# Loading one tile transposed by DMA instead of transposing it on TensorE, at the start of a gated attention and feed-forward kernel

## The chip, the cores and the metric

The kernel runs on one core of a Trainium2 chip. The metric is device microseconds of one execution; medians of several executions are given with their range. The whole program takes about 274 us, and the change touches its first 8 us, so most effects below are some tenths of a microsecond, or about a thousandth of the time.

## The reference

```python
x = A_x                                             # 2048 x 640, bf16
g = sigmoid((x * gate_w).sum(-1, keepdims=True))
# A: linear attention, 32 heads of 20
q, k, v = split(x @ wqkv)                           # wqkv 640 x 1920
phi = lambda t: where(t > 0, t + 1, exp(t)) + 1e-6
o = (phi(q) @ (phi(k).T @ v)) / (phi(q) @ sum(phi(k)))      # per head
a = o @ wo
# B: gated feed-forward, F = 1728
b = (gelu(x @ w_gate) * (x @ w_up)) @ w_down
out = g * a + (1 - g) * b
```

## The kernel before

x is cut into 16 tiles of 128 rows. Keys and queries need x transposed (`xT`), 128 columns (one chunk `k` of 5) at a time. Tiles 0 and 1 are loaded plainly and transposed on TensorE (`T`, through PSUM and a VectorE copy). Tiles 2 to 15 come transposed by DMA (`load_xT`).

```python
NXN = 2          # tiles transposed on TensorE
NQ = 4           # tiles whose keys and queries are computed apart, at the start
# ... cut
P.op("act", lambda e: e.dma_start(touch[...], ...))      # a tiny first DMA
load_x(0)                    # SyncE's queue, as all without "act"
load_wk(0)
load_x(1, "act")             # ScalarE's queue
load_wk(1)
load_wk(3)
P.op("act", lambda e: e.activation(eg[:, 0:1], zero, ACT.Exp), ...)
load_wk(2, "act")
load_wk(4, "act")
P.op("dve", lambda e: e.memset(gw_sb, 0.0), writes=[r_gw])
dma_in(gw_sb[0:5, :], gate_w..., [r_gw], eng="act")
for i in range(NXN, NQ):
    load_xT(i)               # DMA transpose, SyncE's queue
for k in range(KC):
    load_wq(k)
for i in range(NQ, NT):
    load_xT(i)
# ... cut: the rest of x, the feed-forward weights

# TensorE, in this order (warm(n, w): n matmuls of w columns on constants)
warm(5, 512); warm(1, 128)
T(0, [0], 7); T(0, [1, 2, 3, 4], 6)
warm(6, 128)
KM(0, [0])                   # keys of tile 0, chunk 0: 512 + 128 columns
T(1, [0], 7); T(1, [1, 2, 3, 4], 6)
warm(3, 128)
KM(1, [0])
for k in (1, 2, 3):
    KM(0, [k]); KM(1, [k])
gate_col()
KM(0, [4]); KM(1, [4])
# keys of tiles 2 and 3, queries of tiles 0 to 3
# ... cut
```

Then come keys and queries of tiles 4 to 15 together. Each tile's PSUM result is turned into phi by ScalarE (exp) and VectorE (min and add, then add and max, for keys in two parts):

```python
def phi(half, dst, r_dst, banks, cuts):          # in KQ(i), i = 4 to 15
    P.op("act", exp of 640 columns, reads=banks, ...)
    if half: P.op("act", tanh of one column, ...)
    P.op("dve", min and add, ...)
    for c0, c1, bk in cuts:
        P.op("dve", add and max, reads=bk + [r_e[m]], writes=[r_dst])
```

After tile 15 TensorE starts the products of keys and x ("k-v products" here), summed over the 16 tiles. Their steady part starts with line 599.

Of the kernel before, what the change touches and what calls it, by code (L numbers as in the profile page):

```python
# [20 lines left out]
EPS = 1e-6  # L21
XW = 656

NXN = 2
NQ = 4


# [135 lines left out]
def bass_gated_mix__linear_attn_block__geglu_ffn__prompt_kernel(  # L163
# [63 lines left out]
    with (  # L227
# [8 lines left out]
        with contextlib.ExitStack() as stack:  # L236
            dma_sems = [stack.enter_context(nc.semaphore("s_in%d" % i)) for i in range(n_dma_in)]

            P = _Plan(["pe", "act", "dve", "pool", "sp"])
# [9 lines left out]
            def new_dma_key():  # L249
                k = "in%d" % dma_next[0]  # L250
                dma_next[0] += 1
                return k

            def v16(o, n):
                return pool[:, o:o + n]
# [10 lines left out]
            xT = v16(R_XT, KC * S).rearrange("p (k s) -> p k s", k=KC)  # L266

            wkq = v16(R_WK, KC * WW).rearrange("p (k w) -> p k w", k=KC)
            wk = wkq[:, :, 0:640]
# [38 lines left out]
            r_xT = [P.sb("xT%d" % i, R_XT, R_XT + KC * S) for i in range(NT)]  # L308
            r_xTa = [P.sb("xTa%d" % i, R_XT, R_XT + S) for i in range(NXN)]
            r_wk = [P.sb("wk%d" % k, R_WK + k * WW, R_WK + k * WW + 640) for k in range(KC)]  # L310
# [29 lines left out]
            def dma_in(dst, src, writes, reads=(), eng="sp"):  # L340
                P.op(eng, lambda e, dst=dst, src=src: e.dma_start(dst, src),
                     reads=reads, writes=writes, dma=new_dma_key())
# [3 lines left out]
            def load_x(i, eng="sp"):  # L346
                dma_in(x_aug[:, i, 0:640], A_x[0, i * 128:(i + 1) * 128, :], [r_xn[i]], eng=eng)

            def load_wk(k, eng="sp"):
                dma_in(wk[:, k, :], A_wqkv[k * 128:(k + 1) * 128, 640:1280], [r_wk[k]], eng=eng)  # L350

            def load_wq(k, eng="sp"):
                dma_in(wq[:, k, 0:640], A_wqkv[k * 128:(k + 1) * 128, 0:640], [r_wq[k]], eng=eng)
# [3 lines left out]
                 writes=[P.res("touch")], dma=new_dma_key())  # L357
            load_x(0)
            load_wk(0)
            load_x(1, "act")  # L360
            load_wk(1)
            load_wk(3)

            zero = nc.const_aps.tensor(0.0, (128, 1), F32)
            P.op("act", lambda e: e.activation(eg[:, 0:1], zero, ACT.Exp), writes=[r_eg[0]])
            load_wk(2, "act")
            load_wk(4, "act")
            P.op("dve", lambda e: e.memset(gw_sb, 0.0), writes=[r_gw])
            dma_in(gw_sb[0:5, :], gate_w.rearrange("(k p) -> k p", p=128), [r_gw], eng="act")
            def load_xT(i, after=()):  # L370
                P.op("sp", lambda e: e.dma_start_transpose(xT[:, :, i * 128:(i + 1) * 128],
                                                           A_x[0, i * 128:(i + 1) * 128, :]),
                     reads=list(after), writes=[r_xT[i]], dma=new_dma_key())

            for i in range(NXN, NQ):
                load_xT(i)
            for k in range(KC):
                load_wq(k)
            for i in range(NQ, NT):
                load_xT(i)  # L380
            dma_in(x_aug[:, NXN:8, 0:640],
                   A_x[0, NXN * 128:8 * 128, :].rearrange("(i p) w -> p i w", p=128), r_xn[NXN:8])
            dma_in(x_aug[:, 8:NT, 0:640],
# [4 lines left out]
            for c in range(NHC):  # L388
# [9 lines left out]
                 reads=[r_ones], writes=[r_ident])  # L398
# [16 lines left out]
            def warm(count, n):  # L415
                def fn(e):
                    last = None
                    for w in range(count):
                        last = e.matmul(ps[:, 4, 0:n], one_l, one_r[:, 0:n], start=True, stop=True)  # L419
                    return last  # L420
                P.op("pe", fn, writes=[bank[4]])
# [4 lines left out]
            def slot(n):  # L426
                return SLOTS[n % 4]

            def T(i, ks, tb):
                def fn(e):  # L430
                    last = None
                    for n, k in enumerate(ks):
                        last = e.transpose(psb[:, tb, n * 128:(n + 1) * 128],
                                           x_aug[:, i, k * 128:(k + 1) * 128], ident)
                    return last
                P.op("pe", fn, reads=[r_xn[i], r_ident], writes=[bank[tb]])
                P.op("dve", lambda e: e.tensor_copy(
                    xT[:, ks[0]:ks[-1] + 1, i * 128:(i + 1) * 128],
                    psb[:, tb, 0:len(ks) * 128].rearrange("p (k s) -> p k s", k=len(ks))),
                    reads=[bank[tb]], writes=[r_xTa[i] if ks[0] == 0 else r_xT[i]])  # L440
# [4 lines left out]
            def KM(n, ks):  # L445
                i = seq[n][1]
                b0, b1 = slot(n)

                def fn(e):
                    last = None  # L450
                    for k in ks:
                        lhs = xT[:, k, i * 128:(i + 1) * 128]
                        e.matmul(ps[:, b0, :], lhs, wk[:, k, 0:512], start=(k == 0), stop=(k == KC - 1))  # L453
                        last = e.matmul(ps[:, b1, 0:128], lhs, wk[:, k, 512:640],  # L454
                                        start=(k == 0), stop=(k == KC - 1))
                    return last
                P.op("pe", fn, reads=[r_xTa[i] if i < NXN and ks == [0] else r_xT[i]] + [r_wk[k] for k in ks],
                     writes=[bank[b0], bank[b1]])
# [37 lines left out]
            def gate_col():  # L496

                P.op("pe", lambda e: e.matmul(ps[:, 7, 0:5], gw_sb, ident[:, 0:5], start=True, stop=True),
                     reads=[r_gw, r_ident], writes=[bank[7]])
                P.op("dve", lambda e: e.tensor_copy(wq[:, :, 640:641], ps[:, 7, 0:5].unsqueeze(2)),  # L500
                     reads=[bank[7]], writes=[r_gcol])
# [3 lines left out]
            warm(1, 128)  # L505
            T(0, [0], 7)
            T(0, [1, 2, 3, 4], 6)
            warm(6, 128)
            KM(0, [0])
            T(1, [0], 7)  # L510
            T(1, [1, 2, 3, 4], 6)
            warm(3, 128)
            KM(1, [0])
            for k in (1, 2, 3):
                KM(0, [k])
                KM(1, [k])
            gate_col()
            for k in (4,):
                KM(0, [k])
                KM(1, [k])  # L520
            ALLK = list(range(KC))
            for n in range(2 * NQ):
                if n in (2, 3):
# [45 lines left out]
            for i in range(NQ, NT):  # L569
                KQ(i)  # L570
                if i == 4:
                    late_constants()
            P.op("dve", lambda e: e.tensor_scalar(gg, eg, 0.5, 0.5, ALU.mult, ALU.add),
                 reads=r_eg, writes=[r_g])
            P.op("dve", lambda e: e.tensor_scalar(omg, eg, -0.5, 0.5, ALU.mult, ALU.add),
                 reads=r_eg, writes=[r_omg])
# [7 lines left out]
                 reads=[r_omg], writes=[r_od], dma=new_dma_key())  # L584
# [44 lines left out]
            def ME(g):  # L629
# [6 lines left out]
                for c in cs:  # L636
# [8 lines left out]
                 reads=r_pk[0:2], writes=[r_tmp[0]])  # L645
            for i in range(2, NT):
                P.op("dve", lambda e, i=i: e.tensor_tensor(zacc, zacc, pk[i], ALU.add),  # L647
                     reads=[r_tmp[0], r_pk[i]], writes=[r_tmp[0]])
# [283 lines left out]
```

## Time and profile before

| | us |
|---|---|
| median of the first three executions | 273.77 (273.75 to 274.64) |
| span of the traced execution | 272.7 |
| TensorE busy | 269.8 (99%) |

The profile's page gives busy times in its first part and, in its fourth, the chain of work that ended last, as shares of the span.

```profile
PE 269.8 (99%) x1379; PEld 128.7 (47%) x1379; DVE 141.0 (52%) x249; ACT 75.9 (28%) x132; POOL 30.0 (11%) x28
...
PE 98%; DVE 1%; ACT 0%; issue 0%; DVEq 0%
```

TensorE is nearly always busy and nearly all of the chain. The timeline view shows the start: start in us, duration, engine, line, operation. Line 433 is a transpose, 419 a warm-up, 453 the first half of a keys matmul pair.

```profile
3.02 0.73 PE L433 MATMUL ps<-pool 128*128 128x128 bf16 x5
...
3.55 0.85 PE L419 MATMUL ps<-const-bfloat16-1.0 128*128 128x128 bf16 x6
...
4.52 0.50 PE L453 MATMUL ps<-pool 128*128 128x512 bf16 x1
...
4.91 0.44 PE L433 MATMUL ps<-pool 128*128 128x128 bf16 x5
...
5.19 0.34 PE L419 MATMUL ps<-const-bfloat16-1.0 128*128 128x128 bf16 x3
...
5.45 0.39 PE L453 MATMUL ps<-pool 128*128 128x512 bf16 x1
...
5.74 0.38 PE L453 MATMUL ps<-pool 128*128 128x512 bf16 x1
...
7.93 0.38 PE L453 MATMUL ps<-pool 128*128 128x512 bf16 x1
```

Tile 1's transposes and three warm-ups stand in the stream from 4.91 to 5.45. From there, pairs follow every 0.27 us, and 7.93 is the first keys matmul of tile 2. For the cost of a DMA transpose, the view by windows compares 16 to 20 us, mostly transposes, with 25 to 47 us, bulk loads. The columns are the stretch, its length, the busy time and instructions of TensorE, its weight loads, VectorE, ScalarE and GpSimd, the clock, the DMA engines' busy share and GB/s.

```profile
16.00:20.00 4.00, 4.00 (x24) 2.11 (x22) 3.32 (x8) 1.50 (x4) 0.00 (x0) 1.00 0.61 125
25.00:47.00 22.00, 22.00 (x124) 11.85 (x122) 19.37 (x41) 11.76 (x24) 0.00 (x0) 1.00 1.02 365
```

### The profile page before, as it was taken

How to read it: one execution, taken by the hardware profiler on the slowest of the kernel's cores; microseconds unless marked ns; L12 is line 12 of the kernel's file. 1: busy time of each engine (PE TensorE's matmuls, PEld its weight loads, DVE VectorE, ACT ScalarE, POOL GpSimd, SP SyncE). 2: the span in 40 equal slices, each digit the busy share in tenths (PEclk: the TensorE clock that was granted, in tenths of full speed). 3: DMA queues.
4: the chain of work that ended last, by engine and by line, in shares of the span. 5: the costliest groups of instructions: out<-in, count | busy, mean ns of one | idle time of the engine just before them, and what ended most of it. 6: DMA issues, size and time to landing. Idle time of an engine off the chain costs nothing.

```text
span 272.7 us, 3467 instructions
## 1 busy us (share of the span) xinstructions
PE 269.8 (99%) x1379; PEld 128.7 (47%) x1379; DVE 141.0 (52%) x249; ACT 75.9 (28%) x132; POOL 30.0 (11%) x28
## 2 busy tenths in 40 slices
PE   8999999999999999999999999999999999999997
PEld 4555555444445444444444444444444444444444
DVE  2688989897233335999999999634210000000200
ACT  2455554210422453232222233224011122121021
POOL 5000000003240002242332422000000000000000
DMA  7976999300210011612121231263031110110221
GB/s 211 210 111 137 384 402 377 52 3 18 59 22 0 23 50 50 190 36 49 26 48 24 48 48 28 60 218 108 2 77 38 41 38 19 38 41 19 58 60 38
DMA packets 42208, 23.61 MB, mean 87 GB/s; under 512 B 31567, under 2 KB 40783, under 8 KB 42063
## 3 DMA queue, kind: packets, MB, share of 16 engines
q1 hardware_dynamic: 41717, 22.89, 31.2%
q10 hardware_dynamic: 474, 0.49, 0.5%
q8 instruction: 11, 0.18, 0.3%
q14 instruction: 6, 0.05, 0.1%
HBM read 13.83 MB, written 2.63 MB: 60 GB/s over the span
## 4 chain that ended last, share of the span: by engine, by line
PE 98%; DVE 1%; ACT 0%; issue 0%; DVEq 0%
PE ps L703 41%; PE ps L867 23%; PE ps L542 11%; PE ps L599 6%; PE ps L846 4%; PE ps L453 2%; PE ps L468 2%; PE ps L814 2%; PE ps L681 2%; PE ps L602 1%; PE ps L419 1%; PE ps L827 1%; PE ps L724 1%; PE ps L742 0%; PE ps L469 0%; PE ps L454 0%
## 5 line engine op out<-in xcount | busy, mean ns | idle before, releaser
L703 PE MATMUL ps<-pool 128*128 128x512 bf16 x520 | 113.7, 379 | 0.0
L703 PEld LDWEIGHTS ps<-pool 128*128 128x128 bf16 x520 | 50.5, 98 | 60.0
L867 PE MATMUL ps<-pool 128*128 128x512 bf16 (+2 forms) x306 | 62.7, 367 | 0.0
L709 ACT ACTIVATE pool<-ps 128x512 f32<-128x512 f32 x52 | 31.0, 597 | 73.1 <-PE ps L703 73.1
L711 DVE TENSOR_TENSOR pool<-ps,pool 128x512 bf16<-128x512 f32 x52 | 34.7, 689 | 31.7 <-PE ps L703 30.3
L867 PEld LDWEIGHTS ps<-pool 128*128 128x128 bf16 x306 | 29.2, 98 | 33.4 <-issue 0.4
L850 DVE TENSOR_TENSOR pool<-ps,pool 128x512 bf16<-128x512 f32 x4 | 2.8, 692 | 61.5 <-PE ps L846 61.5
L542 PE MATMUL ps<-pool 128*128 128x512 bf16 (+1 forms) x180 | 32.7, 344 | 0.0
L757 POOL TENSOR_TENSOR pool<-pool 128x640 f32<-128x640 bf16 x16 | 22.4, 1404 | 72.9 <-DVE pool L759 65.9
L874 ACT ACTIVATE pool<-ps,pool 128x512 bf16<-128x512 f32 (+1 forms) x16 | 10.9, 680 | 68.6 <-PE ps L867 68.6
L542 PEld LDWEIGHTS ps<-pool 128*128 128x128 bf16 x180 | 17.6, 98 | 15.0
L561 DVE SCALAR_TENSOR_TENSOR pool<-ps,pool 128x128 bf16<-128x128 f32 (+2 forms) x36 | 21.7, 603 | 2.5 <-DVE pool L558 0.5
L552 ACT ACTIVATE pool<-ps 128x640 bf16<-128x640 f32 x24 | 16.9, 703 | 16.1 <-DVE pool L561 9.0
L599 PE MATMUL ps<-pool 128*128 128x512 bf16 x78 | 19.4, 379 | 0.0
L767 DVE TENSOR_TENSOR pool<-pool 128x640 bf16<-128x640 bf16 x16 | 13.2, 825 | 0.6
L765 DVE TENSOR_SCALAR pool<-pool 128x32 f32<-128x32 f32 x16 | 12.8, 801 | 0.6
L759 DVE TENSOR_REDUCE pool<-pool 128x32 f32<-128x640 f32 x16 | 12.9, 809 | 0.0
L647 DVE TENSOR_TENSOR pool<-pool 128x640 f32<-128x640 f32 x14 | 11.6, 826 | 0.5
L846 PE MATMUL ps<-pool 128*128 128x512 bf16 x52 | 11.6, 380 | 0.0
L649 POOL PARTITION_ALL_REDUCE pool<-pool x1 | 4.0, 3971 | 61.2 <-DVE pool L647 61.2
L599 PEld LDWEIGHTS ps<-pool 128*128 128x128 bf16 x78 | 7.0, 98 | 7.2
L558 DVE TENSOR_SCALAR pool<-pool 128x640 bf16<-128x640 bf16 x24 | 7.8, 325 | 2.0 <-ACT pool L552 0.8
(70 smaller groups left out, 127.4 us busy)
## 6 DMA issues: line engine op xcount, KB each, us to landing
out_dram<-pool SPq DMA_DIRECT2D x19, 128.0 KB, 1.7
pool<-in_B_w_gate_dram SPq DMA_DIRECT2D x1, 2080.0 KB, 14.4
pool<-in_B_w_up_dram SPq DMA_DIRECT2D x1, 2080.0 KB, 19.0
pool<-in_A_wqkv_dram SPq DMA_DIRECT2D x8, 160.0 KB, 3.2
pool<-in_A_x_dram SPq DMA_DIRECT2D x1, 1280.0 KB, 8.8
pool<-in_B_w_down_dram SPq DMA_DIRECT2D x1, 1120.0 KB, 6.3
pool<-omg_row SPq DMA_DIRECT2D x1, 1024.0 KB, 4.8
pool<-in_A_x_dram SPq DMA_DIRECT2D x1, 960.0 KB, 5.9
```

The source lines that it names most:

```text
L542: last = e.matmul(ps[:, b + p, 0:c1 - c0], xT[:, k, i * 128:(i + 1) * 128], wkq[:, k, c0:c1], start=(k == 0), stop=(k == KC - 1))
L552: P.op("act", lambda e: e.activation(e_buf[m], ps_flat[:, o:o + 640], ACT.Exp), reads=banks, writes=[r_e[m]])
L561: P.op("dve", lambda e, c0=c0, c1=c1: e.scalar_tensor_tensor(dst[:, c0:c1], ps_flat[:, o + c0:o + c1], 1.0 + EPS, e_buf[m][:, c0:c1], ALU. ...
L599: last = e.matmul(ps[:, b, :], pk[i][:, c * 128:(c + 1) * 128], x_aug[:, i, 0:512], start=(i == 0), stop=(i == NT - 1))
L703: last = e.matmul(ps[:, b, :], w[:, k, fc * 128:(fc + 1) * 128], xT[:, k, j * 512:(j + 1) * 512], start=(k == 0), stop=(k == KC - 1))
L709: P.op("act", lambda e: e.activation(ge[n], ps[:, gb, :], ACT.Gelu_apprx_tanh), reads=[bank[gb]], writes=[r_ge[n]])
L711: P.op("dve", lambda e: e.tensor_tensor(hT[fc][:, j * 512:(j + 1) * 512], ps[:, ub, :], ge[n], ALU.mult), reads=[bank[ub], r_ge[n]], write ...
L757: P.op("pool", lambda e: e.tensor_tensor(tmp[n], pq[i], z_b, ALU.mult), reads=[r_pq[i], r_zb], writes=[r_tmp[n]])
L759: P.op("dve", lambda e: e.tensor_reduce(den[n], tmp[n].rearrange("p (h d) -> p h d", h=32), AX.X, ALU.add), reads=[r_tmp[n]], writes=[r_de ...
L767: P.op("dve", lambda e: e.tensor_tensor(pq[i].rearrange("p (h d) -> p h d", h=32), pq[i].rearrange("p (h d) -> p h d", h=32), den[n].unsqu ...
L846: last = e.matmul(ps[:, b, :], wd[:, fc, 512:640], hT[fc][:, j * 512:(j + 1) * 512], start=False, stop=(fc == NFC - 2), skip_group_check=True)
L867: last = e.matmul(ps[:, pb, 0:c1 - c0], lhs, rhs, start=False, stop=(q == len(rows) - 1), skip_group_check=True)
```

## The change

The intent: TensorE bounds the kernel, so take tile 1's transposes and the three warm-ups that follow them from its stream, and let the DMA do them. Tile 1's transpose goes third on SyncE's queue. wk chunks 1 and 2 go to ScalarE's queue, which no longer carries x tile 1. TensorE runs tile 0's keys for chunks 0 to 2 first, while tile 1 arrives.

```diff
-NXN = 2
+NXN = 1
@@ loads (SyncE's queue unless "act")
             load_x(0)
             load_wk(0)
-            load_x(1, "act")
-            load_wk(1)
+            load_xT(1)
             load_wk(3)
+            load_wk(4)
+            load_wk(1, "act")
+            load_wk(2, "act")
 ... the exponential that loads ScalarE's table
-            load_wk(2, "act")
-            load_wk(4, "act")
-            for i in range(NXN, NQ):
+            for i in range(2, NQ):
                 load_xT(i)
@@ TensorE
             T(0, [0], 7)
             T(0, [1, 2, 3, 4], 6)
-            warm(6, 128)
-            KM(0, [0])
-            T(1, [0], 7)
-            T(1, [1, 2, 3, 4], 6)
-            warm(3, 128)
-            KM(1, [0])
-            for k in (1, 2, 3):
+            warm(2, 128)
+            for k in range(3):
                 KM(0, [k])
+            for k in range(3):
                 KM(1, [k])
+            KM(0, [3])
+            KM(1, [3])
             gate_col()
-            for k in (4,):
-                KM(0, [k])
-                KM(1, [k])
+            KM(0, [4])
+            KM(1, [4])
```

(The helper `load_xT` moves up and helpers get an unused argument.) VectorE loses two copies, because T(1) is gone. And tile 1 of x is now moved twice: the later products need it untransposed too, so the bulk load of x that begins at tile `NXN` grows from 960 to 1120 KB (issued at about 25 us).

More of the change, by code (lines that the diff above doesn't have):

```diff
@@ L347, in load_x, with load_wk, load_xT @@
                 dma_in(x_aug[:, i, 0:640], A_x[0, i * 128:(i + 1) * 128, :], [r_xn[i]], eng=eng)
-            def load_wk(k, eng="sp"):
-                dma_in(wk[:, k, :], A_wqkv[k * 128:(k + 1) * 128, 640:1280], [r_wk[k]], eng=eng)
+            def load_wk(k, eng="sp", after=()):
+                dma_in(wk[:, k, :], A_wqkv[k * 128:(k + 1) * 128, 640:1280], [r_wk[k]], reads=after, eng=eng)
+            def load_xT(i, after=()):
+                P.op("sp", lambda e: e.dma_start_transpose(xT[:, :, i * 128:(i + 1) * 128],
+                                                           A_x[0, i * 128:(i + 1) * 128, :]),
+                     reads=list(after), writes=[r_xT[i]], dma=new_dma_key())
             def load_wq(k, eng="sp"):
@@ L359, in bass_gated_mix__linear_attn_block__geglu_ffn__prompt_kernel @@
             load_wk(0)
-            load_x(1, "act")
-            load_wk(1)
+            load_xT(1)
             load_wk(3)
+            load_wk(4)
+            load_wk(1, "act")
+            load_wk(2, "act")
             zero = nc.const_aps.tensor(0.0, (128, 1), F32)
             P.op("act", lambda e: e.activation(eg[:, 0:1], zero, ACT.Exp), writes=[r_eg[0]])
-            load_wk(2, "act")
-            load_wk(4, "act")
             P.op("dve", lambda e: e.memset(gw_sb, 0.0), writes=[r_gw])
             dma_in(gw_sb[0:5, :], gate_w.rearrange("(k p) -> k p", p=128), [r_gw], eng="act")
-            def load_xT(i, after=()):
-                P.op("sp", lambda e: e.dma_start_transpose(xT[:, :, i * 128:(i + 1) * 128],
-                                                           A_x[0, i * 128:(i + 1) * 128, :]),
-                     reads=list(after), writes=[r_xT[i]], dma=new_dma_key())
-            for i in range(NXN, NQ):
+            for i in range(2, NQ):
                 load_xT(i)
```

## The prediction

> **What bounds the kernel now.** TensorE is busy 99% of the 272.7 us span (page, part 1) and 98% of the chain that ended last (part 4), at clock 1.00. The change touches only the first 8 us; the timeline there: x tile 0 transposed on TensorE from 3.02; six warm-up matmuls 3.55-4.40; keys of tile 0, chunk 0, at 4.52; tile 1's five transposes 4.91-5.19 and three warm-ups to 5.45; then keys matmuls without a gap, one pair (512+128 columns) each 0.27 us; keys of tiles 0 and 1 end at 7.93.
>
> Landings (DMA view by window, issue plus time to landing): x0 3.0, wk0 4.35, x1 4.5, wk1 5.5, wk2 5.7, wk3 6.25, wk4 6.5, xT2 7.15, xT3 7.65, wq0 8.2, wq4 10.6. The 0.36 us wait before 4.52 is put down to DVE, whose copy ended at 3.59: it is really wk0. From 5.45 on TensorE bounds, with data 0.2 to 0.8 us ahead.
>
> **What the change does.** It removes tile 1's transposes (0.28 us) and three warm-ups (0.26) from TensorE's stream, and two DVE copies (0.65, off the path). If data kept up, keys would end 0.54 us earlier, and all later TensorE work with them. Four other warm-ups go from a wait for wk0: worth nothing.
>
> It adds a DMA transpose of 160 KB as SyncE's third transfer. Its issue holds the queue 1.2 to 1.3 us (source view; a plain load 0.45), so everything from wq on, and xT2 and xT3, is issued about 1.3 us later; wk3 goes from 2.15 to about 3.0, wk4 to about 3.4. It also costs more DMA time: in 16-20 us, transposes only, the engines moved 125 GB/s at a share of 0.61; bulk loads in 25-47 us moved 365 at 1.02. Estimate from these: 0.8 us of all engines for a tile against 0.46. The Trainium skill ("Advanced Engine Details and Errata", X-Bar Transpose) calls trn2's transposes as fast as regular DMAs; this trace disagrees. Moving wk1 and wk2 to ScalarE's queue saves issue time only (skill, "DMA: Bandwidth & Descriptors", Issuing engines are not separate DMA queues); the share is already 1.0 in 3-5 us.
>
> **Critical path after.** Estimates from those landings: wk0 and wk1 4.4-4.6; wk2 about 5.4; xT1, issued at 1.7, about 5.6 (3.6 to 4.5 after issue: 5.3 to 6.2); wk3 6.3; wk4 6.7; xT2 7.4; xT3 8.5; wq4 11.9. Keys of tile 0 chunks 0-1 run from 4.5, chunk 2 waits until 5.4, tile 1 until about 5.7; then seven pairs, gap-free: end about 7.65 against 7.93. xT2, xT3 and wq then still arrive just in time. So about half of 0.54 us returns as a wait for xT1 or wk2: gain near 0.3 us.
>
> **Prediction: 273.5 us**, 80% range 272.9 to 274.2. Faster by over 2%: 0.5%; within 2%: 99%; slower: 0.5%.
>
> **Right if** no tile 1 transposes appear; TensorE idles about 0.5 us before 4.5 and some tenths between 4.9 and 5.8, released by DMA; keys of tiles 0 and 1 end at 7.4-7.8; later stages keep their lengths.
>
> **Wrong if** xT1 lands after 6.0 (no gain or a loss); xT2, xT3 or wq are late (waits between 7.6 and 13); or the thinner warm-up leaves the clock low: here 128 columns took 107 ns before 4.4 and 56 ns after 4.9, the step that the skill ("TensorE: Matmul & The Clock Gate", Part 1) describes. Delayed, keys pairs would take 0.53 us and 1 us or more is lost. If wk2 and xT1 land by 5.2, the gain is 0.5 to 0.9.

## More of the kernel before

The timeline at 47 to 50 us:

```profile
47.46 0.70 ACT L552 ACTIVATE pool<-ps 128x640 bf16<-128x640 f32 x1 [1.19 <-PE ps L542]
...
48.20 0.33 DVE L558 TENSOR_SCALAR pool<-pool 128x640 bf16<-128x640 bf16 x1 [0.41 <-ACT pool L552]
...
48.62 0.59 PE L609 MATMUL ps<-pool 128*128 128x512 bf16 x2
48.63 0.82 DVE L561 SCALAR_TENSOR_TENSOR pool<-ps,pool 128x640 bf16<-128x640 f32 x1
49.05 0.69 PE L614 MATMUL ps<-pool 128*128 128x512 bf16 x2
...
49.58 0.59 PE L599 MATMUL ps<-pool 128*128 128x512 bf16 x2
```

From line 609 to line 599 it takes 0.96 us here. VectorE's add and max for tile 14 ends at 49.45, and line 614's second half waits for it. The modelled durations (0.69 for two matmuls) hide the wait. The view of waits from 16 to 60 us names it, and another: who waited for whom, us in total, times, longest.

```profile
PEld ps L614 <- DVE pool L561: 0.6, 1, 0.6
DVE pool L561 <- DVE pool L558: 0.5, 1, 0.5
```

The second line is VectorE idle for half a microsecond between two of its own instructions. That happens at 34.6 us, in tile 9, between min-and-add and the second half's add-and-max.

## The result, and the profile after

| | before | changed |
|---|---|---|
| median, us | 274.11 | 273.90 |
| range, six executions each | 273.75 to 274.69 | 273.57 to 274.06 |
| span of the traced execution | 272.7 | 272.6 |

The ratio is 0.9988, with a 95% interval of 0.9973 to 1.0003: the same within 2%, and not clear of noise. A ratio is the mean time of one kernel's fast runs over that of the other's fast runs in the same rounds, so it is not quite the ratio of the medians quoted.

Page of the changed kernel, parts one and four:

```profile
PE 267.6 (98%) x1341; PEld 127.9 (47%) x1367; DVE 140.8 (52%) x247; ACT 75.9 (28%) x132; POOL 30.0 (11%) x28
...
PE 96%; DMA 1%; SPq 1%; issue 1%; DVE 0%
```

(The 1341 matmuls against 1367 weight loads are records missing from the trace.) The chain now runs through SyncE's queue and a DMA. The timeline of the start:

```profile
3.03 0.73 PE L433 MATMUL ps<-pool 128*128 128x128 bf16 x5
...
4.45 0.58 PE L453 MATMUL ps<-pool 128*128 128x512 bf16 x1 [0.48 <-DMA pool<-in_A_wqkv_dram]
...
4.93 0.51 PE L453 MATMUL ps<-pool 128*128 128x512 bf16 x1
...
5.34 0.38 PE L453 MATMUL ps<-pool 128*128 128x512 bf16 x1
...
5.61 0.38 PE L453 MATMUL ps<-pool 128*128 128x512 bf16 x1
...
7.27 0.38 PE L453 MATMUL ps<-pool 128*128 128x512 bf16 x1
...
8.12 0.39 PE L453 MATMUL ps<-pool 128*128 128x512 bf16 x1 [0.42 <-DMA pool<-in_A_x_dram]
```

Three things are to be seen:

- Tile 1's transpose was in time: the fourth pair (5.61) does not wait.
- The first two pairs took 0.48 and 0.41 us instead of 0.27: the clock was still slow. In before, warm-ups and transposes had filled that time.
- The last pair of tile 1 begins at 7.27 and would end near 7.54, 0.39 us ahead of before. Tile 2's keys start only at 8.12, because they wait for tile 2's transpose. Before had them at 7.93. (The 0.42 us that the view shows counts from the modelled end of the last matmul; from 7.54 to 8.12 it is 0.58 us.)

So this trace's start is 0.19 us later than before's, and yet the span is 0.1 us shorter. The rest is at the start of the k-v products:

```profile
47.22 0.70 ACT L549 ACTIVATE pool<-ps 128x640 bf16<-128x640 f32 x1 [0.78 <-DVE pool L558]
...
48.39 0.82 DVE L558 SCALAR_TENSOR_TENSOR pool<-ps,pool 128x640 bf16<-128x640 f32 x1
...
48.80 0.59 PE L606 MATMUL ps<-pool 128*128 128x512 bf16 x2
...
49.23 0.43 PE L611 MATMUL ps<-pool 128*128 128x512 bf16 x2
49.50 0.59 PE L596 MATMUL ps<-pool 128*128 128x512 bf16 x2
```

From line 606 to 596 (609 to 599 in before) it takes 0.70 us instead of 0.96. VectorE is done with tile 14 at 49.21. Its waits from 16 to 60 us no longer have the half microsecond of VectorE waiting for itself; of the two lines shown of before, one is left, and shorter:

```profile
PEld ps L611 <- DVE pool L558: 0.2, 1, 0.2
```

From here on I cut every trace into three stretches: A, from the start to the first keys matmul of tile 2; B, from there to the steady part of the k-v products; C, the rest. B holds no instruction of TensorE, VectorE or ScalarE that the diff touches; only some of its loads are issued later, and one is larger.

### The profile page after: what moved, and what is told of

Its sections match the earlier page's. It is cut to its first block, busy times and chain, and to the rows that moved or that the text cites. A ratio compares the mean times of both kernels' runs of the same rounds, so it can differ in the third digit from the quotient of the medians.

```text
span 272.6 us, 3416 instructions
## 1 busy us (share of the span) xinstructions
PE 267.6 (98%) x1341; PEld 127.9 (47%) x1367; DVE 140.8 (52%) x247; ACT 75.9 (28%) x132; POOL 30.0 (11%) x28
## 4 chain that ended last, share of the span: by engine, by line
PE 96%; DMA 1%; SPq 1%; issue 1%; DVE 0%
PE ps L700 41%; PE ps L864 23%; PE ps L539 12%; PE ps L596 6%; PE ps L843 4%; PE ps L468 2%; PE ps L811 2%; PE ps L678 2%; PE ps L599 1%; DMA pool<-in_A_x_dram 1%; PE ps L453 1%; PE ps L824 1%; SPq L341 1%; PE ps L721 1%; SPq L353 0%
```

## The experiments

Each kernel was checked for correctness on the chip. All passed, also no_xT2_wait, which is wrong: the check does not see the keys of one tile of sixteen computed from another tile. "Before" in each job ran beside it on the same chip.

| run | median us (range) | ratio to before, 95% | A ends | B | C |
|---|---|---|---|---|---|
| before, first trace | 274.11 (273.75 to 274.69) | | 7.93 | 41.64 | 223.1 |
| changed, first trace | 273.90 (273.57 to 274.06) | 0.9988 (0.9973 to 1.0003) | 8.12 | 41.38 | 223.1 |
| before_again | 273.99 (273.82 to 274.67) | 0.9997 (0.9983 to 1.001) | 8.67 | 41.64 | 223.1 |
| after_again | 273.73 (273.40 to 274.27) | 0.9985 (0.9971 to 1.0) | 7.90 | 41.38 | 223.1 |
| warm6 | 273.97 (273.54 to 274.02) | 0.9987 (0.9973 to 1.0) | 8.24 | 41.39 | 223.1 |
| wk34_act | 276.57 (275.28 to 277.81) | 1.0086 (1.0062 to 1.011) | 10.48 | 41.54 | 223.1 |
| before_dve2 | 273.76 (273.53 to 274.56) | 0.9993 (0.9977 to 1.0009) | 8.35 | 41.53 | 223.1 |
| after_dve2 | 274.05 (273.87 to 274.27) | 1.0 (0.9988 to 1.0013) | 8.23 | 41.39 | 223.1 |
| shift_before | 281.42 (281.23 to 282.14) | 1.0275 (1.0257 to 1.0292) | 15.46 | 41.64 | 223.1 |
| shift_after | 281.36 (281.22 to 281.41) | 1.0267 (1.0252 to 1.0282) | 15.54 | 41.38 | 223.1 |
| before_moved | 273.86 (273.72 to 275.08) | 0.9993 (0.9978 to 1.0008) | 8.32 | 41.39 | 223.1 |
| after_restored | 274.11 (273.81 to 275.92) | 1.0006 (0.9983 to 1.0028) | 8.07 | 41.63 | 223.1 |
| no_xT2_wait | 273.82 (273.46 to 274.15) | 0.9984 (0.9972 to 0.9996) | 8.27 | 41.39 | 223.1 |
| lean_before | 274.28 (273.67 to 275.15) | 1.0002 (0.9986 to 1.0017) | 8.52 | 41.39 | 223.1 |

C is the same in all. B takes one of few values, to 0.01 us: it belongs to the program. A varies from execution to execution of the same program. (In wk34_act the clock was slow at the beginning of B.) So two questions remain: what sets B, and what limits A.

### Both kernels again: before_again and after_again

No edit.

> The kernel before, unchanged, as a control. Ratio 1.000 within 0.1%. First theory of the later stages: the 0.5 us gap that VectorE had at 34.6 us in the first trace of before, and the 0.3 us wait of TensorE at 49.1 us that follows from it, is an accident of that one execution; then this trace lacks both, and TensorE starts the k-v products' steady part (first line after the first tile's) at about 49.3 us instead of 49.58, so the span is about 272.4. Rival: they belong to the kernel, and both come again. The step of the clock (128 columns from 107 to 56 ns) should fall near 4.7 us again if it is tied to the program, elsewhere if its window runs freely.

> The changed kernel again, as a control. Ratio 0.9988 as found, 0.998 to 1.000. Keys of tile 2 start at 8.1 us again, after a wait for the DMA transpose of tile 2 of about 0.5 us, whichever theory of its cause holds. TensorE starts the steady part of the k-v products at 49.5 us. If the slow clock until about 5.2 us is chance it differs from the first trace by some tenths and keys of tiles 0 and 1 end at 7.2 to 7.8.

My first theory of B fell. VectorE's pause and TensorE's wait came again in before_again, 0.73 us later, with everything else, and at the same instruction. They belong to the kernel. A was 8.67 instead of 7.93: chunk 0 came later (first keys matmul at 4.73) and the clock stayed slow longer (transposes and warm-ups of tile 1 took from 5.21 to 6.07 instead of 4.91 to 5.45). In after_again the clock was slow longer than in the first trace too (the third pair still took 0.43 us), but A ended at 7.90, since the wait for tile 2 swallowed it. Expected for A were 8.1 us and a wait of about 0.5; TensorE in fact waited only 0.1 us for tile 2, which landed a little earlier here.

### Six warm-ups instead of two: warm6

```diff
-            warm(2, 128)
+            warm(6, 128)
```

> The changed kernel with six instead of two short warm-up matmuls, as before. Theory C, the thin warm-up delays the fast clock: keys pairs of chunks 0 and 1 take 0.27 to 0.4 us instead of 0.48 and 0.41, and keys of tiles 0 and 1 end about 0.3 us earlier, at 7.2 to 7.3 us. But if tile 2's transpose sets the pace (theories A and B) its keys still start at 8.1 us and the time is that of the changed kernel within 0.1 us. If the clock's step comes at its own time, nothing changes at all.

In this execution chunk 0 arrived late (first pair at 4.99) and the clock was fast by then: all pairs took 0.27 us. Tile 1's transpose, not tile 2's, was waited for (0.30 us before 6.30), and A ended at 8.24. The time is that of the changed kernel, so nothing shows that a thin warm-up held the gain back; one trace cannot say whether six warm-ups made the clock rise earlier.

### More of wk on the other queue: wk34_act

```diff
-            load_wk(3)
-            load_wk(4)
             load_wk(1, "act")
             load_wk(2, "act")
+            load_wk(3, "act")
+            load_wk(4, "act")
```

> The changed kernel with wk chunks 3 and 4 on ScalarE's queue too, so SyncE issues the transposes of tiles 2 and 3 about 1.1 us earlier (3.05 and 4.35 us instead of 4.14 and 5.45). Theory A, SyncE's issue holds tile 2 back: it lands at 6.9 to 7.3 us instead of 8.04, chunks 3 and 4 by 7.0, keys of tile 2 start at 7.5 to 7.6 without a wait, and the program is about 0.55 us shorter than the changed kernel (ratio to before about 0.997). Theory B, the DMA engines are full: the last of chunk 3, chunk 4 and tile 2 still lands at 7.9 or later, keys of tile 2 start at 8.0 or later, and the time is that of the changed kernel.

Neither theory foresaw a loss of 2.4 us. The timeline of this kernel:

```profile
5.09 0.38 PE L453 MATMUL ps<-pool 128*128 128x512 bf16 x1
...
7.05 0.39 PE L453 MATMUL ps<-pool 128*128 128x512 bf16 x1 [1.53 <-DMA pool<-in_A_x_dram]
...
7.79 0.63 PE L453 MATMUL ps<-pool 128*128 128x512 bf16 x1
...
8.33 0.63 PE L453 MATMUL ps<-pool 128*128 128x512 bf16 x1
```

TensorE waits 1.53 us for tile 1, and after that pause the clock falls back: pairs take about 0.53 us until about 10.5, and the granted clock is 0.50 from 7.4 to 10.8 us. Four of the six executions have a mean clock of 0.994, as this one. The other two (1.000), at 275.28 and 276.06 us, are still 1.1 and 1.9 us above the median of before beside it, 274.18. The view of DMA issues (the last number is us from issue to landing) shows why, first the changed kernel's two transposes, tile 1 issued at 1.71 and tile 2 at 4.14 us:

```profile
pool<-in_A_x_dram SPq DMA_TRANSPOSE x1, 3.8
...
pool<-in_A_x_dram SPq DMA_TRANSPOSE x1, 3.9
```

and those of wk34_act, issued at 1.71 and 3.06 us:

```profile
pool<-in_A_x_dram SPq DMA_TRANSPOSE x1, 5.3
...
pool<-in_A_x_dram SPq DMA_TRANSPOSE x1, 4.9
```

Tile 1 landed at 7.0 instead of 5.5. Tile 2, issued 1.1 us earlier, landed at 7.9 instead of 8.0. So an earlier issue bought tile 2 next to nothing: the whole set of transfers up to tile 2 was complete at 7.9 us instead of 8.0, which is what theory B said, that the engines are full. (From 3 to 8 us their busy share was 1.06 in the changed kernel and 1.14 here.) Tile 1's transpose on SyncE's queue lost 1.5 us to the plain loads that ran beside it on ScalarE's; chunks 3 and 4, issued about 0.9 us and 1.0 us earlier, gained nothing by it and landed about 0.4 us later. Theory A, that SyncE's issue time holds tile 2 back, is refuted, although the chain of the changed kernel names SyncE's issues.

### Two more instructions on VectorE: before_dve2 and after_dve2

```diff
             P.op("dve", lambda e: e.memset(gw_sb, 0.0), writes=[r_gw])
+            P.op("dve", lambda e: e.memset(gw_sb, 0.0), writes=[r_gw])
+            P.op("dve", lambda e: e.memset(gw_sb, 0.0), writes=[r_gw])
```

> The kernel before with two more small memsets at the head of VectorE's stream (it is idle there), so that every later VectorE instruction stands two places later. In both traces of before, VectorE pauses 0.43 us ahead of the 64th instruction record (counting from 1), which the changed kernel's three normal traces lack; TensorE then waits 0.27 us more at the start of the k-v products. Theory F, the pause hangs on the place in VectorE's stream, which the change shifts by two by dropping two copies: here it goes too; from the first key matmul of tile 2 to the steady part of the k-v products it takes 41.38 us as in the changed kernel instead of 41.65, and the ratio to before is about 0.999. Rival: the pause comes from what else runs at that moment (the order of loads); then it stays, 41.65 us, ratio 1.000.

> The changed kernel with two more small memsets at the head of VectorE's stream, which puts its later instructions at the places that they have in before. Theory F: the pause of about 0.43 us comes back at the same instruction (tile 9, before the second half's max), TensorE waits 0.25 us again at the k-v products, 41.65 us from keys of tile 2 to their steady part, and the ratio to before rises from 0.9986 to about 0.9995 to 1.000. Rival, the prologue itself made the gain: no pause, 41.38 us, ratio 0.9986 as the changed kernel.

The pause obeyed theory F, and B did not. Waits of before_dve2 from 16 to 60 us: the pause is gone, and TensorE still waits.

```profile
PEld ps L616 <- DVE pool L563: 0.5, 1, 0.5
```

Waits of after_dve2 in the same stretch: the pause is back, and TensorE's wait has hardly grown against the 0.2 us that the changed kernel has.

```profile
DVE pool L560 <- DVE pool L557: 0.5, 1, 0.5
...
PEld ps L613 <- DVE pool L560: 0.3, 1, 0.3
```

B was 41.53 in before_dve2 (expected 41.38) and 41.39 in after_dve2 (expected 41.65). Half of the cause was missing. In the records of the traces I then compared each tile's phi with TensorE's start of that tile. VectorE keeps one distance (5.84 us from the first KQ matmul, after taking out 2.708 us per tile) until it pauses in tile 9, then is 0.42 us late, and makes up 0.06 us per tile. In before a second delay came in tile 14, the last tile but one: 0.31 us against after_dve2, which has the first delay alone. It began on ScalarE, ahead of the exponential of tile 14's second half (47.46 in the lines of before above; its semaphore wait had ended at 47.11).

The records of both engines, with their semaphore waits counted as records of their own, show what the two places have in common. Idle time ahead of the 64th record of the stream, in us:

| trace | VectorE, 64th record | idle | ScalarE, 64th record | idle |
|---|---|---|---|---|
| before, before_again, shift_before, after_restored | add and max, after a semaphore wait | 0.45 to 0.47 | exp, after a semaphore wait | 0.35 |
| before_dve2 | min and add, after an instruction | 0.10 | exp, after a semaphore wait | 0.35 |
| after_dve2 | add and max, after a semaphore wait | 0.46 | tanh, after an instruction | none |
| changed, after_again, warm6, shift_after, no_xT2_wait | add and max, after an instruction | 0.03 | tanh, after an instruction | none |
| wk34_act | add and max, after an instruction | 0.03 | a semaphore wait itself | (that wait) |
| before_moved, lean_before (later runs) | min and add, after an instruction | 0.10 | a semaphore wait itself | (that wait) |

The same instructions in other tiles start 0.04 us after their semaphore wait. (The 0.10 us ahead of that min-and-add is the ordinary gap there.) So theory G: each engine pauses ahead of its 64th record, and the pause shows only where that record directly follows a semaphore wait; elsewhere the previous instruction, still running, would cover it (this last part is not tested). Record 128 of both streams follows a semaphore wait in before too and starts no later after it than its neighbours do (0.43 us on VectorE), so no second such pause is seen there (on ScalarE it could hide in the 2.13 us of idle time). The change took two instructions from VectorE and one from ScalarE and so moved both.

### All loads held back, clock warm: shift_before and shift_after

```diff
+            r_delay = P.res("delay")
+            for d in range(13):          # GpSimd memsets of free space, 0.63 us each
+                P.op("pool", memset(...), writes=[...] + ([r_delay] if d == 12 else []))
             P.op("act", touch load, reads=[r_delay])
             load x tile 0, reads=[r_delay]
@@
-            warm(5, 512)
+            warm(26, 512)
+            warm(8, 512, after=[r_delay])
```

> The kernel before with all loads held back by about 8 us (13 memsets on GpSimd, which the first loads wait for) while TensorE runs 29 more long warm-ups, so that its clock is up before x arrives in every execution. Times from the first load's issue as in before. Theory D, the free phase of the clock's step makes before's spread (keys of tile 2 started at 7.93 us in one trace with an early step, 8.67 in one with a late step): here keys of tile 2 start 7.0 to 7.15 us after the issue of the first load (7.14 in the first trace of before) in every execution, and the ten times spread by less than 0.5 us instead of 1.0. Rival, landings make the spread: it stays 1.0. The time itself is 8 to 9 us longer.

> The changed kernel, held back and warmed in the same way. Theory D: with a fast clock from the start the keys of tiles 0 and 1 are done at 6.7 us after the first load's issue, but tile 2's transpose lands 7.2 us after it as before, so keys of tile 2 start at 7.1 to 7.35, no earlier than in shift_before (a loss of 0 to 0.3 us in the prologue), and only the pause of VectorE (0.27 us) is in its favour: the two differ by less than 0.3 us. Rival E, TensorE work taken away is what gains: keys of tile 2 start at least 0.4 us earlier than in shift_before, and with the pause it is 0.7 us faster.

With a fast clock from the start, tile 2's keys began 7.19 us after the first load's issue in shift_before (15.46 less 8.27, just outside the expected 7.0 to 7.15) and 7.28 in shift_after (15.54 less 8.26). The changed start was 0.09 us later. In shift_after TensorE waited for tile 1 and tile 2, 0.6 us together:

```profile
PE ps L457 <- DMA pool<-in_A_x_dram: 0.6, 2, 0.3
```

That refutes rival E: with the clock out of the way, taking half a microsecond of work from TensorE gained nothing in this stretch, and the medians differ by 0.06 us where E forecast 0.7. B kept its two values, 41.64 and 41.38. About the spread the result is mixed. Only four times each came out. Three of shift_before lie within 0.24 us, the fourth is 282.14; shift_after's four lie within 0.19. So the clock is not all of the spread. Landings vary too: wk chunk 1 landed at 5.5 us in the first trace of before, and at 6.1 in before_dve2, where TensorE waited 0.36 us for it.

### Both streams moved: before_moved and after_restored

```diff
             P.op("dve", lambda e: e.memset(gw_sb, 0.0), writes=[r_gw])    # three times, as above
             dma_in(gw_sb[0:5, :], gate_w..., [r_gw], eng="act")
+            P.op("act", lambda e: e.activation(eg[:, 1:2], zero, ACT.Exp), writes=[r_eg[1]])
```

> The kernel before with two small memsets more at the head of VectorE's stream and one tiny exponential more at the head of ScalarE's, all in idle time: later instructions stand two and one places later. Theory G: both engines pause ahead of their 64th record where that record follows a semaphore wait (VectorE 0.46 us at tile 9, ScalarE 0.36 us at tile 14 in before, 0.04 otherwise); the change moved both streams and so lost both pauses. Then here both are gone, from the first key matmul of tile 2 to the steady part of the k-v products it is 41.38 us as in the changed kernel, not 41.65 as in before or 41.54 as with VectorE moved alone, and the ratio to before is 0.999. Rival: ScalarE's pause comes from the order of the loads; then it stays and the stretch is 41.54.

> The changed kernel with two memsets more on VectorE and one tiny exponential more on ScalarE, so that both streams have before's places again. Theory G: both pauses come back, the stretch from keys of tile 2 to the steady part of the k-v products is 41.65 us, and the time rises by 0.27 us against the changed kernel, to a ratio to before of 0.9995 to 1.0005: what the prologue itself gives is then left alone, -0.2 to 0 us. Rival: 41.38 us and 0.9986.

Theory G held, in both directions. Waits of before_moved, 16 to 60 us:

```profile
PEld ps L617 <- DVE pool L564: 0.2, 1, 0.2
```

and of after_restored:

```profile
PEld ps L614 <- DVE pool L561: 0.6, 1, 0.6
DVE pool L561 <- DVE pool L558: 0.5, 1, 0.5
```

before_moved has the loads and the TensorE order of before and the B of the changed kernel (41.39). after_restored has the change and the B of before (41.63). The rival (the order of loads makes the pauses) falls. With VectorE's pause alone B is 41.39, with ScalarE's alone 41.53, with both 41.64: VectorE's comes in tile 9, five tiles ahead of tile 14, whose phi the products wait for, and is nearly made up by then; ScalarE's comes in tile 14 itself, and adds to what is left of the first.

The times agree in direction (before_moved 0.9993, after_restored 1.0006), but their intervals hold 1. They are widened by one execution each, 275.08 and 275.92. Nor do the times of the other kernels follow B alone: after_dve2 has the short B and 1.0000, lean_before (below) the short B and 1.0002. What the pauses cost is read from B, not from these times.

### Without the wait for tile 2: no_xT2_wait (wrong)

```diff
             def KM(n, ks):
-                i = seq[n][1]
+                i = 1 if n == 2 else seq[n][1]      # keys of tile 2 from tile 1's x
```

> The changed kernel, wrong on purpose: keys of tile 2 are computed from tile 1's transpose, so TensorE does not wait for tile 2's transpose (all transfers stay). If that wait alone takes back what the prologue gained, keys of tile 2 start right after those of tile 1, at 7.5 us with an early step of the clock and 7.8 to 8.2 with a late one, tile 3's transpose (8.85 us) then costs 0 to 0.1 us, and the time falls by 0 to 0.5 us against the changed kernel, 0.2 us in the median (ratio to before about 0.998). If the clock is what holds the prologue back, nothing changes.

The ratio, 0.9984, lies within 0.0004 (0.1 us) of the changed kernel's two. In its trace the clock was slow until about 6.8 us, so five pairs took 0.44 to 0.54 us, and A ended at 8.27 without any wait for x. after_dve2 had the same clock and the wait in its program, and ended A at 8.23. In such executions the wait costs nothing, because the clock has already used the time. The expected 0.2 us do not show, but no changed kernel ran beside it, and a difference of that size lies within the intervals.

### An attempt to beat both: lean_before

```diff
 (before_moved, and)
-            warm(3, 128)          # ahead of KM(1, [0])
```

> The kernel before with both streams moved (as before_moved) and without the three short warm-ups ahead of tile 1's first key matmul: the likeliest version to beat both. The pauses are gone (41.38 us). The warm-ups fill the wait for tile 1's copy when the clock is fast (gain 0), and cost 0.3 us when it is slow. Keys of tile 2 start at 7.9 us with an early step, 8.35 with a late one; the median is 0.3 to 0.4 us below before (ratio 0.9987), level with the changed kernel or 0.1 better.

It did not beat anything: 1.0002. B was 41.39 as expected. In its trace chunk 0 came late (4.92 us) and A ended at 8.52. No version is shown to beat the changed kernel.

## Why the prediction was right or wrong

- **The time** was right: 273.90 us lies in 272.9 to 274.2, and the gain, 0.2 us in the medians, is near the 0.3 forecast. It came by another way than the one predicted, so the close match is in part luck; and the range also holds the median of before itself (274.11), so a time inside it does not show that the mechanism was right.
- **"about half of 0.54 us returns as a wait for xT1 or wk2"** failed. In the first trace tile 1 landed at 5.5 us (forecast 5.6) and was not waited for. What was waited for was tile 2, 0.42 us. It was forecast to land at 7.4, just in time, and landed at about 8.05; a late tile 2 is one of the conditions that the prediction names under "Wrong if", and it came true. The mis-sized term is the landing of tile 2: 0.9 us later than in before (7.15), where 0.25 was forecast. My own estimate of a transpose's extra DMA time was 0.34 us, so the forecast was too low even by that. That estimate rests on one trace, and on the lowest share of the twelve traces not shifted in time: before_dve2 has 0.92 at 121 GB/s in the same 16 to 20 us, which by the same reckoning makes 1.2 us for a transposed tile instead of 0.8. And from 3 to 8 us the DMA engines were as busy in before (1.11) as in the changed kernel (1.06) but moved 311 GB/s against 252; the missing 0.3 MB would take 0.9 us at before's rate (an estimate from these numbers). So the dearer transpose fits the whole delay. wk34_act shows that an earlier issue of tile 2 does not undo it. The later issue and the dearer transpose are not fully separated.
- **"Delayed, keys pairs would take 0.53 us"** came true in part: the first two pairs took 0.48 and 0.41 us, and in other executions up to five took 0.44 to 0.54. But the loss is not added to the waits. It runs while the data is on its way (after_dve2 and no_xT2_wait).
- **"later stages keep their lengths"** was wrong, and this is the point that matters most. B, which the diff does not touch, became 0.26 us shorter in the changed kernel. It is the only part of the gain that the runs pin down, and before_moved has it without the change.
- **Keys of tiles 0 and 1 end at 7.4 to 7.8**: right in the first trace (about 7.54) and in after_again.
- **What the start itself gives** stays open, but it is little. Ends of A with before's loads and order are 7.93, 8.67, 8.35 and 8.32 (four traces), with the changed ones 8.12, 7.90, 8.23 and 8.07. The means differ by 0.24 us in favour of the change, but the ranges overlap, and the run that isolates it in time, after_restored, gave 1.0006 with an interval of 0.9983 to 1.0028. With the clock warm the changed start was 0.09 us slower in one trace each. All times together narrow it: if the B of its program is taken from every execution's time, what is left differs between the changed start (24 executions) and before's (57) by -0.07, -0.12, 0.25 and 0.10 us in the four jobs (minus is faster), 0.04 us slower on average, with an interval of -0.13 to 0.24 by resampling (an estimate; it takes B as the same in all executions of a program, as it was in the traces). So the start itself gains nothing that can be measured, and B's 0.26 us is all of the gain that is found. What these fit, without proving it, is that the change trades TensorE work, which a slow clock stretches, for a wait that is about the same in every execution. The narrower range of the changed kernel's times (273.40 to 274.27 in twelve executions; before, 273.75 to 274.76 in seventeen of the same two jobs) points the same way, but after_restored, with the same start, had the widest range of these (273.81 to 275.92).
- **What the pauses are** also stays open. Shown is where they fall, and that moving a stream by one or two instructions removes or restores them. Every B here comes from a profiled execution; whether the pauses occur when nothing is recorded, no run shows.

## What to carry to other kernels

Where two versions differ by a thousandth, cut both traces into stretches and compare those that the edit does not touch: a gain there belongs to something else, such as the place of instructions in another engine's stream, and can be had without the change. Before taking work from the busiest engine, ask what its next instruction waits for; here the data was only just in time, so the freed half microsecond turned into waits. Transposing loads took more of the DMA engines than plain loads of the same bytes, and plain loads issued earlier on the other queue made the first of them later still (tile 1 in wk34_act, 5.3 us to landing instead of 3.8).

## What the Trainium skill lacked or had wrong

- No page has the pause ahead of the 64th record of VectorE's and ScalarE's streams. It was 0.45 to 0.47 us on VectorE and 0.35 us on ScalarE where that record follows a semaphore wait, in every trace that had the case, and absent otherwise. "Runtime: NRT & Kernel Launch", Instruction fetch mechanics, calls the fetching of instructions hidden; whether these pauses are fetches, no run here shows.
- "Advanced Engine Details and Errata", X-Bar Transpose, calls trn2's transposing DMAs as fast as regular ones. In the trace of before the engines moved 125 GB/s at a share of 0.61 in 16 to 20 us, mostly transposes, and 365 GB/s at 1.02 in 25 to 47 us, bulk loads. That makes about 205 against 358 GB/s at a full share (an estimate from these four numbers). In the other traces the share in 16 to 20 us was higher (0.92 at 121 GB/s in before_dve2), which makes the rate lower still.
- "DMA: Bandwidth & Descriptors", Issuing engines are not separate DMA queues, says that spreading DMAs over queues saves only issue time. The shared engines are as it says (tile 2, issued 1.1 us earlier, landed 0.1 us earlier). But which queue a load is on also decides who waits: with chunks 3 and 4 on the other queue, tile 1's transpose took 5.3 us from issue to landing instead of 3.8 (chunks 3 and 4 were also issued about 1 us earlier; the two are not separated).
- "TensorE: Matmul & The Clock Gate", Part 1, says that the window of the clock runs freely, and these runs agree: keys pairs were fast from 4.83 us on in one trace and slow until about 6.8 us in others of nearly the same program. Its rule counts idle gaps above about 3.4 us as harmful; in wk34_act a wait of 1.53 us, ended at 7.05 us, was followed by slow pairs (about 0.53 us) and a granted clock of 0.50 from 7.4 us on. In the 3.4 us before that TensorE was busy for 1.3 us.
